# One-hot tables of a token router: five wide VectorE instructions per two chunks in place of twelve on GpSimd

## The chip, the cores and the metric

One core of a Trainium2 chip runs the whole program. Its engines each work through their own instruction queue in order and wait for each other by semaphores: TensorE (PE, and PEld for its weight loads), VectorE (DVE), ScalarE (ACT), GpSimd (POOL) and SyncE (SP, which here only starts DMAs). The metric is the device time of one execution in microseconds; the kernel before takes 539.12 us (median of three, 538.48 to 539.36).

## The reference

Three layers follow each other. The first is an mLSTM recurrence over 2 x 8 heads of 768 steps, the second a mixture of eight experts of which each token uses two, the third an MLP with a gated activation.

```python
for t in range(S):                       # B, H, S, D = 2, 8, 768, 40
    m_new = np.maximum(f_gate[:, :, t] + m, i_gate[:, :, t])
    f_stab, i_stab = np.exp(f_gate[:, :, t] + m - m_new), np.exp(i_gate[:, :, t] - m_new)
    C = f_stab * C + i_stab * outer(v_t, k_t);  n = f_stab * n + i_stab * k_t
    y[:, :, t] = sigmoid(o_t) * (C @ q_t) / np.maximum(np.abs(n @ q_t), 1.0)
x = y as 1536 tokens of 320
noisy = x @ w_gate + np.log1p(np.exp(x @ w_noise)) * noise
top2 = np.argpartition(-noisy, 2, axis=1)[:, :2]       # weights: softmax of the two
for e in range(8):                                     # F = 1024
    out[mask] += top2_w * (np.maximum(x[mask] @ w1[e], 0) @ w2[e])
h = out @ w_in;  result = (h * np.clip(h + 3, 0, 6) / 6) @ w_out      # 2048 wide
```

## The kernel before, in words

The 768 steps of both batches are cut into 12 chunks of 128 rows (64 steps of each batch). The loop from line 1077 walks over the chunks: it reads the state (`inter`), adds to it (`state`), makes scores two chunks ahead (`scores`), multiplies with the values (`values`, line 339), transposes the finished rows (`xpose`, line 412) and computes the router's logits (line 426). VectorE multiplies scores and decays into `P` (line 292), updates the state `Sb` (line 328), and finishes the chunk in `y`, `den`, `rd` and `x` (lines 358 to 384). GpSimd makes the decayed state `Sd` (line 301) and the gated output `od` (line 369).

For each pair of chunks a generator `route(m)`, m = 0 to 5, picks the two experts of each token and gives each token a place in its expert's list. It is cut by `yield` into small pieces; every call of `step()` in the main program runs each living generator up to its next yield, so the number of yields decides where its instructions stand in the engines' queues, between those of the main program. Some pieces wait until a counter `spot` has moved on.

A route counts tokens per expert by matmuls (lines 488 to 491), adds the base of each expert (`pe`, line 511), and turns the result into a slot number `sl`. The last part enters the tokens into a table of slots. The slot's low seven bits `lh[:, 0]` choose one of 128 rows, the others one of 32 columns. `LO` is the one-hot of the row (four choices of 128 each), `HV` the one-hot of the column times the token's number, in two parts (`pcol`, the row in the chunk, and `nval`, the chunk's first token). Four matmuls at line 562 multiply the two, and line 564 adds the result into `slot`. After m = 3 and after m = 5 the table is turned into indices `idx` (line 567), from which GpSimd gathers the tokens of the experts (`gather`, line 818).

Routes 0 to 4 make `LO` and `HV` on GpSimd, with twelve instructions whose comparands are per-partition scalars in `lf`, a float32 copy of `lh`. Route 5 makes them on VectorE with wide instructions that broadcast both operands. Routes 4 and 5 run beside the first expert unit, whose first layer is `L1` (line 891, evicted by ScalarE at 894 and VectorE at 897) and whose second is `L2` (lines 927 to 932). The weights come as float32 and are split in two parts, on ScalarE (line 641) and VectorE (line 642). From the first unit on TensorE goes through the experts and then the MLP.

Of the kernel before, what the change touches and what calls it, by code (L numbers as in the profile page):

```python
# [13 lines left out]
BF = mybir.dt.bfloat16  # L14
# [4 lines left out]
OP = mybir.AluOpType  # L19
# [3 lines left out]

B, H, S, D = 2, 8, 768, 40
NT = 12
DM = H * D
E = 8
# [39 lines left out]
def mlstm_moe_mlp(ctx, tc, qk, kv, on, gf, gf4, wg, nz, w1, w2, w_in, w_out, cf, cb, ci, out):  # L67
    nc = tc.nc
    V, A, G, T = nc.vector, nc.scalar, nc.gpsimd, nc.tensor
    const = ctx.enter_context(tc.tile_pool(name="const", bufs=1))  # L70
# [47 lines left out]
    def kv_part(n):  # L118
        kvt[n] = att.tile([128, H * (D + V1)], F32, name="kv", bufs=4)
        return kvt[n], kv[n]  # L120

    def load_qk(n, eng=nc.sync):
        for a in qk_parts(n):
            eng.dma_start(*a)

    def load_kv(n, eng=nc.sync):
        eng.dma_start(*kv_part(n))

    def load_on(n):
        nc.sync.dma_start(ont[:, n:n + 2], on[:, n:n + 2])  # L130
# [64 lines left out]
    def later_exponents():  # L195
        exponents(g64[:, 1], g64[:, 0], m64, 64, 1, R[:, 0], R[:, 1], R[:, 2])
        for sp in range(3):
            G.dma_start(RWG[sp * 32:sp * 32 + 16, 2:6].rearrange("p c x t -> p (c x t)"),
                        R[:, sp].rearrange("p c x t -> p (c x t)"))
        pre_cm.__exit__(None, None, None)  # L200
# [20 lines left out]
    iota128, pcol, nval = cft[:, 147:275], cft[:, 275:276], cft[:, 276:288]  # L221
# [21 lines left out]
    def step(k=1):  # L243
        for _ in range(k):
            for g_ in list(gens):
                if next(g_, "end") == "end":
                    gens.remove(g_)
# [6 lines left out]
    def scores(n, ps_=range(4)):  # L254
        q = QK[n % 4]
        if n not in s4t:
            s4t[n] = (itp if n == 1 else s4p)[:, :, 0:256].rearrange("p x (a t) -> p x a t", a=4)
        s4 = s4t[n]
        for p in ps_:
            for x in range(2):  # L260
                r = slice(64 * x, 64 * x + D)
                for b in range(B):
                    T.matmul(s4[rows[b], x, p, :], q[r, p, 1, rows[b]], q[r, p, 0, rows[b]], start=True, stop=True)
# [24 lines left out]
    def pmul(n):  # L288
        d = Pt[n][1]
        s4 = s4t.pop(n)  # L290
        P = att.tile([128, 8, 64], F32, name="P", bufs=3)
        V.tensor_tensor(P.rearrange("p (x a) t -> p x a t", x=2), s4, d.rearrange("p (x a) t -> p x a t", x=2), OP.mult)
        Pt[n] = P
# [10 lines left out]
    def inter(n, bp=5, two=itp):  # L304
        q = QK[n % 4]
        vv = kvt[n][:, DM:].rearrange("p (h d) -> p h d", h=8)
        pv = bank(bp)[:, 0:8 * V1].rearrange("p (h d) -> p h d", h=8)
        it = two[:, :, 0:4 * V1].rearrange("p x (a c) -> p x a c", a=4)
        for p in range(4 if n else 0):
            for x in range(2):  # L310
                r = slice(64 * x, 64 * x + D)
                for b in range(B):
                    T.matmul(it[rows[b], x, p, :], q[r, p, 0, rows[b]], Sb[r, b, p, :], start=True, stop=True)
        y_ps[n] = (pv, it, vv)

    def state(n):
        Sd = Sds.pop(n, None)
        vv = y_ps[n][2]
        for p in range(4):
            for b in range(B):  # L320
                for x in range(2):
                    h = 4 * x + p
                    T.matmul(stp[64 * x:64 * x + D, b, p, :], kt[n][rows[b], h, :],
                             vv[rows[b], h, :], start=True, stop=True)
        spot[0] += 2
        step(2)
        if n:
            V.tensor_tensor(Sb, Sd, stp, OP.add)
        else:
            V.tensor_copy(Sb, stp)  # L330
        step()
        if n + 2 < NT:
            decay(n + 1)

    def values(n, hs):
        pv, _, vv = y_ps[n]
        for h in hs:
            for b in range(B):
                T.matmul(pv[rows[b], h, :], Pt[n][rows[b], h, :], vv[rows[b], h, :], start=True, stop=True)
# [41 lines left out]
    def norm2(n):  # L381
        o, rd = yt[n]
        x = att2.tile([128, XW], F32, name="x", bufs=4)
        V.tensor_tensor(x[:, 0:DM].rearrange("p (a x d) -> p x a d", a=4, x=2), o.rearrange("p (x a) d -> p x a d", x=2),
                        rd.rearrange("p (x a) -> p x a", x=2)[:, :, :, None].to_broadcast([128, 2, 4, D]), OP.mult)
        A.copy(x[:, DM:XW], x[:, 256:DM])
        xt[n] = x
        nc.sync.dma_start(Xd[n * 128:(n + 1) * 128], x)
# [9 lines left out]
    SLE = const.tile([128, NT, 2], I32, name="SLE")  # L398
    SLY = const.tile([128, NT, 2], I32, name="SLY")
    WAB = const.tile([128, NT, 2], F32, name="WAB")  # L400
    run = const.tile([128, E], BF, name="run")
    V.memset(run, 0.0)
    adj = const.tile([128, E], F32, name="adj")
# [32 lines left out]
    def small(shape, name, dt=F32, bufs=2):  # L436
        return const.tile(shape, dt, name=name, bufs=bufs)

    def route(m):
# [41 lines left out]
        V.tensor_tensor(dl, mx[:, :, 1:2], mx[:, :, 0:1], OP.subtract)  # L481
        wab = WAB[:, 2 * m:2 * m + 2]
        e2 = small([128, 2, 1], "e2")
# [47 lines left out]
        lh = small([128, 2, 4], "lh", I32)  # L531
# [3 lines left out]
        V.scalar_tensor_tensor(lh[:, 1], sli, 7, h1, OP.bitwise_and, OP.bitwise_or)  # L535
        LO = small([128, 4, 128], "LO", BF, 1)
        HV = small([128, 4, 2, 32], "HV", BF, 1)
        if m < NT // 2 - 1:
            lf = small([128, 2, 4], "lf")
            V.tensor_copy(lf, lh)  # L540
            for j in range(4):
                G.tensor_scalar(LO[:, j], iota128, lf[:, 0, j:j + 1], None, OP.is_equal)
                for x, v in enumerate((pcol, nval[:, 2 * m + j // 2:2 * m + j // 2 + 1])):
                    G.tensor_scalar(HV[:, j, x], iota128[:, 0:32], lf[:, 1, j:j + 1], v, OP.is_equal, OP.mult)
        else:
            V.tensor_tensor(LO, iota128[:, None, :].to_broadcast([128, 4, 128]),
                            lh[:, 0, :, None].to_broadcast([128, 4, 128]), OP.is_equal)
            yield
            H = small([128, 4, 32], "H", BF, 1)
            V.tensor_tensor(H, iota128[:, None, 0:32].to_broadcast([128, 4, 32]),  # L550
                            lh[:, 1, :, None].to_broadcast([128, 4, 32]), OP.is_equal)
            yield
            V.tensor_scalar(HV[:, :, 0], H, pcol, None, OP.mult)
            V.tensor_tensor(HV[:, :, 1].rearrange("p (n k) c -> p n k c", n=2), H.rearrange("p (n k) c -> p n k c", n=2),
                            nval[:, 2 * m:2 * m + 2, None, None].to_broadcast([128, 2, 2, 32]), OP.mult)
        at = spot[0]
        yield
        while spot[0] < at + SPI and not now[0]:
# [208 lines left out]
    def w_lo(k=1):  # L767
        for _ in range(k):
            los.pop(0)()
# [33 lines left out]
    for i, u in enumerate(units):  # L803
        u.i = i
        u.g, u.xb = (i - M0) // 3, i % 2 if i < M0 else (i - M0) % 3
        n = len(u.tiles)
# [39 lines left out]
    def combine(u, i):  # L846
        n = 4 * (u.e - 8) + i
        t = ygt[n]
        x = late.tile([128, XW], F32, name="x2", bufs=2)
        A.mul(t[:, 0], t[:, 0], WAB[:, n, 0:1])  # L850
        V.scalar_tensor_tensor(x[:, 0:DM], t[:, 1], WAB[:, n, 1:2], t[:, 0], OP.mult, OP.add)  # L851
        V.scalar_tensor_tensor(x[:, DM:XW], t[:, 1, 256:DM], WAB[:, n, 1:2], t[:, 0, 256:DM], OP.mult, OP.add)
        x2t[n] = x
# [223 lines left out]
    for n in range(NT - 2):  # L1077
        pmul(n + 1)
        step(2)
        inter(n)  # L1080
        state(n)
        if n == 1:
            later_exponents()
            G.tensor_copy(adj, iota8)
        if n + 4 < NT:
            load_qk(n + 4)
        if 0 < n < NT - 3:
            load_kv(n + 3)
        if n % 2 == 0 and n + 2 < NT:
            load_on(n + 2)  # L1090
        if n >= 1:
            norm2(n - 1)
            step()
        w_lo(WL[n] if n < len(WL) else 0)
        scores(n + 2)
        values(n, range(8))
        if n >= 1:
            xpose(n - 1)
        expo(n + 2)
        for _ in range(WD[n] if n < len(WD) else 0):  # L1100
            w_load()
        w_hi(WH[n] if n < len(WH) else 0)
        if n == 1:
            decays(4, NT)
        if n + 3 >= NT:
            dummy(DUM[0], 4)
        if n >= 1:
            logits(n - 1)
        kscale(n + 2)
        if n == 0:  # L1110
            for i in range(3):
                gate(0, i)
        for i in ((0,), (1, 2))[n % 2]:
            gate(n // 2 * 2 + 2, i)
        norm_eg(n)
        step(2)
        norm_pv(n)
        if n >= 2 and n % 2 == 0:
            gens.append(route(n // 2 - 1))
    n = NT - 2  # L1120
# [152 lines left out]
    v, w = hbs  # L1273
# [75 lines left out]
```

## Time and profile before

| | |
|---|---|
| median of three runs | 539.12 us |
| profiled execution | 538.7 us |
| its span, from first to last instruction | 536.9 us |
| TensorE / VectorE / ScalarE / GpSimd busy | 494.1 / 341.1 / 231.7 / 129.2 us |
| mean granted TensorE clock | 0.892 |

Times within the trace are counted from the span's start. The profile's page gives shares over the whole span; the timeline gives the single instructions, with the idle time ahead of each in brackets and the instruction whose end ended it. A busy time of TensorE includes overlap, since its matmuls are pipelined. The granted clock is 1.00 at 2.4 GHz and 0.50 at 1.2 GHz. Line numbers are those of the kernel before, except in rows of the changed kernel, where a line behind the change stands one to three lines elsewhere.

### The profile page before, as it was taken

What the parts mean: (1) busy time and instruction counts of PE and PEld (TensorE: products, weight loads), DVE (VectorE), ACT (ScalarE), POOL (GpSimd) and SP (SyncE); (2) the same over time, 40 slices, a digit from 0 to 9 for tenths busy, and PEclk for the clock granted to TensorE, in tenths of its full rate; (3) what the DMA queues carried; (4) which work ended last, traced back from release to release, by engine and by line L of the source; (5) the groups of instructions that cost most, each with busy time, mean ns of one, the idle gap of its engine ahead of it and who ended that gap; (6) DMA issues with size and microseconds to landing.
All of it is one profiled execution on the core that took longest, in us unless ns stands there. A gap on an engine that the chain in (4) does not pass through costs nothing. (4 is left out here: it accounts for less than half of the span.)

```text
span 536.9 us, 11617 instructions
## 1 busy us (share of the span) xinstructions
PE 494.1 (92%) x4547; PEld 449.1 (84%) x4547; DVE 341.1 (64%) x874; ACT 231.7 (43%) x483; POOL 129.2 (24%) x178
## 2 busy tenths in 40 slices
PE   5799867868699999999999999989999999999996
PEld 2687656646699999999999999979989899899985
DVE  7547766727476587878787877468697434353433
ACT  2346547215254454545454553255564334333322
POOL 2434455263330420202111002377400100000000
PEclk9555555559699999999999999999999999999999
DMA  9858663233277479888988769697722600010011
GB/s 187 206 170 234 167 191 117 71 95 93 79 219 219 151 271 292 290 284 290 273 302 275 267 183 319 205 295 227 241 99 80 214 0 1 1 31 20 13 37 49
DMA packets 41531, 90.76 MB, mean 169 GB/s; under 512 B 5233, under 2 KB 23985, under 8 KB 41473
## 3 DMA queue, kind: packets, MB, share of 16 engines
q1 hardware_dynamic: 34960, 69.07, 41.1%
q0 software_dynamic: 5696, 19.67, 11.9%
q10 hardware_dynamic: 816, 1.25, 1.1%
q8 instruction: 36, 0.59, 0.5%
q14 instruction: 23, 0.18, 0.1%
HBM read 67.16 MB, written 22.68 MB: 167 GB/s over the span
## 5 line engine op out<-in xcount | busy, mean ns | idle before, releaser
L906 DVE SCALAR_TENSOR_TENSOR r<-r,bank 128x512 f32<-128x512 f32 (+1 forms) x56 | 34.2, 611 | 80.1 <-ACT r L905 79.6
L894 ACT ACTIVATE hb<-bank 128x416 fp32r<-128x416 f32 (+2 forms) x80 | 35.6, 446 | 95.9 <-PE bank L891 82.7
L905 ACT ACTIVATE r<-bank,cft 128x512 f32<-128x512 f32 (+1 forms) x56 | 35.0, 626 | 95.5 <-PE bank L891 92.3
L891 PE MATMUL bank<-XH,SB 128*128 128x416 f32 (+3 forms) x280 | 75.6, 340 | 0.3 <-PEq L991 0.3
L891 PE MATMUL bank<-XL,SB 128*128 128x416 f32 (+3 forms) x192 | 66.9, 349 | 0.0
L818 POOL DMA_INDIRECT XG<-Xd,idx x32 | 33.1, 1034 | 127.5 <-PE bank L828 116.7
L927 PE MATMUL bank<-SB,hb 128*128 128x320 f32 x192 | 61.9, 322 | 1.0 <-ACT hb L878 1.0
L927 PE MATMUL bank<-SA,hb 128*128 128x320 f32 x192 | 61.3, 319 | 0.0
L929 PE MATMUL bank<-SA,hb 128*128 128x320 f32 x192 | 59.7, 311 | 0.1
L928 PE MATMUL bank<-SA,hb 128*128 128x320 f32 x192 | 59.6, 310 | 0.0
L929 PE MATMUL bank<-SB,hb 128*128 128x320 f32 x192 | 59.3, 309 | 0.0
L928 PE MATMUL bank<-SB,hb 128*128 128x320 f32 x192 | 59.2, 308 | 0.0
L891 PEld LDWEIGHTS bank<-XH,SB 128*128 128x128 f32 x280 | 50.3, 189 | 4.6 <-issue 0.6
L891 PE MATMUL bank<-XH,SA 128*128 128x416 f32 (+2 forms) x200 | 51.2, 329 | 0.1
L891 PE MATMUL bank<-XL,SA 128*128 128x416 f32 (+2 forms) x120 | 39.3, 329 | 0.1
L891 PEld LDWEIGHTS bank<-XH,SA 128*128 128x128 f32 x200 | 36.5, 196 | 1.9 <-ACT XH L829 0.6
L927 PEld LDWEIGHTS bank<-SB,hb 128*128 128x128 f32 x192 | 36.2, 188 | 2.1 <-ACT hb L878 1.2
L891 PEld LDWEIGHTS bank<-XL,SB 128*128 128x128 f32 x192 | 36.2, 188 | 2.0
L927 PEld LDWEIGHTS bank<-SA,hb 128*128 128x128 f32 x192 | 36.4, 190 | 1.1
L928 PEld LDWEIGHTS bank<-SA,hb 128*128 128x128 f32 x192 | 36.4, 190 | 0.9
L928 PEld LDWEIGHTS bank<-SB,hb 128*128 128x128 f32 x192 | 36.2, 189 | 0.6
L929 PEld LDWEIGHTS bank<-SA,hb 128*128 128x128 f32 x192 | 36.3, 189 | 0.3 <-DVE hb L879 0.3
(225 smaller groups left out, 1113.8 us busy)
## 6 DMA issues: line engine op xcount, KB each, us to landing
raw<-in_w_dram SPq DMA_DIRECT2D x18, 640.0 KB, 4.8
raw<-in_w_dram SPq DMA_DIRECT2D x18, 512.0 KB, 5.6
craw<-in_w_in_dram SPq DMA_DIRECT2D x8, 640.0 KB, 6.4
craw<-in_w_out_dram SPq DMA_DIRECT2D x8, 640.0 KB, 6.4
raw<-in_w_dram SPq DMA_DIRECT2D x18, 256.0 KB, 4.3
qk<-in_qk_dram SPq DMA_DIRECT2D x22, 192.0 KB, 4.3
Yd<-yo SPq DMA_DIRECT2D x24, 160.0 KB, 4.6
kv<-in_kv_dram SPq DMA_DIRECT2D x11, 324.0 KB, 5.0
```

Source lines behind the costliest of these rows:

```text
L818: G.indirect_dma_start(out=XG[0:n, (u.xo + i) % 4, :], out_offset=None, in_=Xd[0:CUT[u.i] * 128] if early else Xd[:, :], in_offset=bass.In ...
L891: T.matmul(p, a, b, start=(i == 0), stop=(i == 7))
L894: A.activation(hb[:, 0:N], p, AF.Relu)
L905: A.activation(r, p, AF.Relu, bias=three)
L906: V.scalar_tensor_tensor(r, r, 6.0, p, OP.min, OP.mult)
L927: T.matmul(p, h, wh, start=s, stop=False)
L928: T.matmul(p, h, wl, start=False, stop=False)
L929: T.matmul(p, hb[:, lo:lo + n], wh, start=False, stop=t)
```

## The change

Routes 0 to 5 now all make the one-hots on VectorE. The ramp that they are compared with is copied once to bfloat16 (`iotab`, on GpSimd in the loop's second pass), `lf` becomes bfloat16, and each of the pieces has its own yield.

```diff
--- before.py
+++ after.py
@@ -398,6 +398,7 @@
     SLE = const.tile([128, NT, 2], I32, name="SLE")
     SLY = const.tile([128, NT, 2], I32, name="SLY")
     WAB = const.tile([128, NT, 2], F32, name="WAB")
+    iotab = const.tile([128, 128], BF, name="iotab")
     run = const.tile([128, E], BF, name="run")
     V.memset(run, 0.0)
     adj = const.tile([128, E], F32, name="adj")
@@ -535,24 +536,20 @@
         V.scalar_tensor_tensor(lh[:, 1], sli, 7, h1, OP.bitwise_and, OP.bitwise_or)
         LO = small([128, 4, 128], "LO", BF, 1)
         HV = small([128, 4, 2, 32], "HV", BF, 1)
-        if m < NT // 2 - 1:
-            lf = small([128, 2, 4], "lf")
-            V.tensor_copy(lf, lh)
-            for j in range(4):
-                G.tensor_scalar(LO[:, j], iota128, lf[:, 0, j:j + 1], None, OP.is_equal)
-                for x, v in enumerate((pcol, nval[:, 2 * m + j // 2:2 * m + j // 2 + 1])):
-                    G.tensor_scalar(HV[:, j, x], iota128[:, 0:32], lf[:, 1, j:j + 1], v, OP.is_equal, OP.mult)
-        else:
-            V.tensor_tensor(LO, iota128[:, None, :].to_broadcast([128, 4, 128]),
-                            lh[:, 0, :, None].to_broadcast([128, 4, 128]), OP.is_equal)
-            yield
-            H = small([128, 4, 32], "H", BF, 1)
-            V.tensor_tensor(H, iota128[:, None, 0:32].to_broadcast([128, 4, 32]),
-                            lh[:, 1, :, None].to_broadcast([128, 4, 32]), OP.is_equal)
-            yield
-            V.tensor_scalar(HV[:, :, 0], H, pcol, None, OP.mult)
-            V.tensor_tensor(HV[:, :, 1].rearrange("p (n k) c -> p n k c", n=2), H.rearrange("p (n k) c -> p n k c", n=2),
-                            nval[:, 2 * m:2 * m + 2, None, None].to_broadcast([128, 2, 2, 32]), OP.mult)
+        yield
+        lf = small([128, 2, 4], "lf", BF)
+        V.tensor_copy(lf, lh)
+        yield
+        V.tensor_tensor(LO, iotab[:, None, :].to_broadcast([128, 4, 128]),
+                        lf[:, 0, :, None].to_broadcast([128, 4, 128]), OP.is_equal)
+        yield
+        H = small([128, 4, 32], "H", BF, 1)
+        V.tensor_tensor(H, iotab[:, None, 0:32].to_broadcast([128, 4, 32]),
+                        lf[:, 1, :, None].to_broadcast([128, 4, 32]), OP.is_equal)
+        yield
+        V.tensor_scalar(HV[:, :, 0], H, pcol, None, OP.mult)
+        V.tensor_tensor(HV[:, :, 1].rearrange("p (n k) c -> p n k c", n=2), H.rearrange("p (n k) c -> p n k c", n=2),
+                        nval[:, 2 * m:2 * m + 2, None, None].to_broadcast([128, 2, 2, 32]), OP.mult)
         at = spot[0]
         yield
         while spot[0] < at + SPI and not now[0]:
@@ -1082,6 +1079,7 @@
         if n == 1:
             later_exponents()
             G.tensor_copy(adj, iota8)
+            G.tensor_copy(iotab, iota128)
         if n + 4 < NT:
             load_qk(n + 4)
         if 0 < n < NT - 3:
```

TensorE's queue, where route 0's slot matmuls (line 562, here the rows with LO) stood, before:

```order
L313 MATMUL itp<-Sb,qk_88 64x41 x16
L323 MATMUL itp<-kv,kt 40x41 x16
L562 LDWEIGHTS LO
L562 MATMUL bank_169<-HV,LO 128x64
L562 LDWEIGHTS LO
L562 MATMUL bank_169<-HV,LO 128x64
L562 LDWEIGHTS LO
L562 MATMUL bank_169<-HV,LO 128x64
L562 LDWEIGHTS LO
L562 MATMUL bank_169<-HV,LO 128x64
L263 MATMUL s4p<-qk_90 64x64 x16
L339 MATMUL bank_1013<-kv,P 64x41 x16
```

and in the changed kernel, at the same place:

```order
L427 MATMUL bank_170<-wgt,xT 32x16 x12
L313 MATMUL itp<-Sb,qk_88 64x41 x16
L323 MATMUL itp<-kv,kt 40x41 x16
L263 MATMUL s4p<-qk_90 64x64 x16
L339 MATMUL bank_1006<-kv,P 64x41 x16
L413 MATMUL bank_1089<-cft,x 128x128 x2
```

and one step later, where line 562 is 559 and line 488 is 489:

```order
L313 MATMUL itp<-Sb,qk_89 64x41 x16
L323 MATMUL itp<-kv,kt 40x41 x16
L559 LDWEIGHTS LO
L559 MATMUL bank_170<-HV,LO 128x64
L559 LDWEIGHTS LO
L559 MATMUL bank_170<-HV,LO 128x64
L559 LDWEIGHTS LO
L559 MATMUL bank_170<-HV,LO 128x64
L559 LDWEIGHTS LO
L559 MATMUL bank_170<-HV,LO 128x64
L489 LDWEIGHTS cbt
```

They moved from between the state matmuls (line 323) and the scores (line 263) of one step to behind the state matmuls of the next one; route 1 likewise. Those of routes 2, 4 and 5 keep their places.

VectorE's queue around the same place, before (line 451 is the route of the next pair, which waits for ScalarE's `u`; 564 the table):

```order
L535 SCALAR_TENSOR_TENSOR lh<-SL,h_978 128x4
L540 CAST lf<-lh 128x8
L377 RECIPROCAL rd<-den 128x8
L292 TENSOR_TENSOR P<-s4p,dd 128x512
L442 COPY zg<-bank_169 128x32
L451 TENSOR_SCALAR w<-u 128x16
L453 SCALAR_TENSOR_TENSOR w<-w,u 128x16
L564 TENSOR_TENSOR slot<-slot,bank_169 128x64
L455 SCALAR_TENSOR_TENSOR w<-zg,w 128x16
L328 TENSOR_TENSOR Sb<-Sd,itp 128x328
```

and in the changed kernel (lines 543 to 551 are the new instructions):

```order
L377 RECIPROCAL rd<-den 128x8
L541 CAST lf<-lh 128x8
L292 TENSOR_TENSOR P<-s4p,dd 128x512
L543 TENSOR_TENSOR LO<-iotab,lf 128x512
L443 COPY zg<-bank_170 128x32
L547 TENSOR_TENSOR H<-iotab,lf 128x128
L452 TENSOR_SCALAR w<-u 128x16
L550 TENSOR_SCALAR HV<-H,cft 128x4x32
L551 TENSOR_TENSOR HV<-H,cft 128x4x32
L454 SCALAR_TENSOR_TENSOR w<-w,u 128x16
L456 SCALAR_TENSOR_TENSOR w<-zg,w 128x16
L328 TENSOR_TENSOR Sb<-Sd,itp 128x328
```

The slot addition has left this stretch, and four wide instructions have come in, two ahead of `w` and two behind it; the addition now stands behind the `P` (line 292) of the next step.

TensorE's queue at the end of the recurrence, route 3, before:

```order
L339 MATMUL bank_1847<-kv,P 64x41 x16
L313 MATMUL s4p<-Sb,qk_90 64x41 x16
L562 LDWEIGHTS LO
L562 MATMUL bank_169<-HV,LO 128x64
L562 LDWEIGHTS LO
L562 MATMUL bank_169<-HV,LO 128x64
L562 LDWEIGHTS LO
L562 MATMUL bank_169<-HV,LO 128x64
L562 LDWEIGHTS LO
L562 MATMUL bank_169<-HV,LO 128x64
L339 MATMUL bank_1920<-kv,P 64x41 x16
L412 MATMUL bank_1989<-cft,x 128x128 x2
```

and in the changed kernel (lines 413 and 427 are lines 412 and 426 of before):

```order
L339 MATMUL bank_1828<-kv,P 64x41 x16
L313 MATMUL s4p<-Sb,qk_90 64x41 x16
L339 MATMUL bank_1901<-kv,P 64x41 x16
L413 MATMUL bank_1958<-cft,x 128x128 x2
L413 MATMUL bank_1958<-cft,x 64x128
L413 MATMUL bank_1977<-cft,x 128x128 x2
L413 MATMUL bank_1977<-cft,x 64x128
L427 MATMUL bank_170<-wgt,xT 32x16 x12
L559 LDWEIGHTS LO
L559 MATMUL bank_170<-HV,LO 128x64
L559 LDWEIGHTS LO
L559 MATMUL bank_170<-HV,LO 128x64
```

The values of the last chunk, two chunks' transposes and one chunk's logits now stand ahead of route 3's slot matmuls.

## Rows read from the trace of the kernel before

**Rows 1.** The page's slices of 13.4 us: granted TensorE clock in tenths.

```profile
PEclk9555555559699999999999999999999999999999
```

**Rows 2.** Two stretches: length, busy (instructions), clock, DMA, GB/s.

```profile
51.90:69.98 18.08, 14.65 (x350) 11.97 (x348) 12.84 (x51) 10.68 (x34) 8.80 (x15) 0.50 0.70 197
200.00:300.00 100.00, 100.00 (x623) 96.79 (x621) 81.67 (x166) 48.56 (x82) 14.69 (x15) 1.00 0.88 288
```

**Rows 3.** Waits, 40 to 160 us: who <- whom: us in total, times, longest.

```profile
PE bank L562 <- POOL HV L544: 24.8, 19, 2.7
...
DVE w L451 <- ACT u L446: 12.1, 5, 2.9
DVE slot L564 <- PE bank L562: 12.1, 4, 5.6
...
DVE pe L511 <- PE bank L491: 3.5, 3, 2.1
...
DVE t L499 <- PE bank L495: 0.7, 1, 0.7
```

**Rows 4.** Groups by form, 40 to 150 us: busy, mean ns, idle.

```profile
L544 POOL TENSOR_SCALAR HV<-cft,lf 128x32 bf16<-128x32 f32 x40 | 18.4, 469 | 0.0
...
L542 POOL TENSOR_SCALAR LO<-cft,lf 128x128 bf16<-128x128 f32 x20 | 12.8, 640 | 8.9 <-DVE lf L540 7.3 <-DVE rd L377 1.1 <-DVE den L374 0.4
```

**Rows 5.** Timeline, 44 to 62 us, TensorE: start, us, instruction [idle].

```profile
51.95 0.77 PE L323 MATMUL itp<-kv,kt 64*40 64x41 f32 x32
...
56.87 1.13 PE L263 MATMUL s4p<-qk 40*64 40x64 f32 x32
```

**Rows 6.** The same timeline, VectorE.

```profile
54.95 0.17 DVE L451 TENSOR_SCALAR w<-u 128x16 f32<-128x16 f32 x1 [2.88 <-ACT u L446]
...
56.98 0.22 DVE L564 TENSOR_TENSOR slot<-slot,bank 128x64 f32<-128x64 f32 x1 [1.61 <-PE bank L562]
```

**Rows 7.** Timeline, 96 to 150 us, TensorE.

```profile
105.28 1.14 PE L313 MATMUL s4p<-Sb,qk 40*64 40x41 f32 x30
...
113.36 1.93 PE L339 MATMUL bank<-kv,P 64*64 64x41 f32 x32
...
123.44 0.38 PE L891 MATMUL bank<-XH,SA 128*128 128x256 f32 x1
...
131.70 0.31 PE L929 MATMUL bank<-SA,hb 128*128 128x320 f32 x1
...
139.33 0.56 PE L891 MATMUL bank<-XH,SA 128*128 128x256 f32 x1
...
141.68 0.61 PE L927 MATMUL bank<-SA,hb 128*128 128x320 f32 x1
...
143.43 0.41 PE L891 MATMUL bank<-XH,SA 128*128 128x256 f32 x1
...
145.40 0.39 PE L927 MATMUL bank<-SA,hb 128*128 128x320 f32 x1
...
146.37 0.29 PE L562 MATMUL bank<-HV,LO 128*128 128x64 bf16 x4
```

**Rows 8.** Timeline, 96 to 150 us, VectorE.

```profile
132.04 1.23 DVE L642 TENSOR_TENSOR SB<-raw,SB 128x1024 fp32r<-128x1024 f32 x1
...
139.51 0.22 DVE L564 TENSOR_TENSOR slot<-slot,bank 128x64 f32<-128x64 f32 x1 [5.91 <-PE bank L491]
...
141.94 0.69 DVE L546 TENSOR_TENSOR LO<-cft,lh 128x512 bf16<-128x512 f32 x1
...
142.87 0.29 DVE L550 TENSOR_TENSOR H<-cft,lh 128x128 bf16<-128x128 f32 x1
...
143.76 0.28 DVE L554 TENSOR_TENSOR HV<-H,cft 128x128 bf16<-128x128 bf16 x1
```

**Rows 9.** Timeline, 96 to 150 us, GpSimd.

```profile
132.31 1.44 POOL L542 TENSOR_SCALAR LO<-cft,lf 128x128 bf16<-128x128 f32 x1 [7.33 <-DVE lf L540]
...
138.21 0.91 POOL L544 TENSOR_SCALAR HV<-cft,lf 128x32 bf16<-128x32 f32 x2
```

## Prediction

> **What bounds the kernel now.** I read four views in this order. First the page's clock by slices [rows 1] and the busy times of two stretches [rows 2]: from 200 to 300 us TensorE is busy for 100.00 of 100.00 us, so the expert stage is bound by TensorE itself, and a microsecond won before it should reach the end of the program. In the recurrence before it nothing is full: in the 18.08 us of one pair of steps TensorE is busy for 14.65 and VectorE for 12.84, at a granted clock of 0.50. Second, the waits between 40 and 160 us [rows 3]: the longest of all is TensorE at line 562 (the four matmuls that add two chunks to the slot table), which waits for GpSimd's HV, 24.8 us in 19 waits. Third, the costs of the two groups it waits for [rows 4]: 40 HV at 469 ns and 20 LO at 640 ns, together 31.2 us for five routes, 6.2 us a route, serial on GpSimd and released by the last one. Fourth, the timelines. TensorE takes its instructions in order: after the state matmuls at 51.95 it could start the scores of a later chunk, and starts them at 56.87 [rows 5], because the slot matmuls stand between. VectorE's slot addition, and behind it the state update Sb, wait as well: 1.61 us here [rows 6], 12.1 us over four routes [rows 3]. Call the routes m = 0 to 5: m = 0 to 2 run inside the recurrence, m = 3 at its end, m = 4 and 5 beside the first expert unit; m = 5 had its one-hots on VectorE already.
>
> **The change, part by part.** It takes 60 instructions off GpSimd and puts four wide ones on VectorE for each of five routes (the fifth, the cast lf, was there). Route m = 5 shows three of the four forms: LO 0.69, H 0.29, the second HV 0.28 us [rows 8]; I count the first HV like the second, so 1.54 us a route. These sources are float32 and int32 and the new ones bfloat16, which no row shows. As bounds I take twice these durations from above, and from below 0.28 for LO as well, since no row of a wide instruction here is shorter; I keep 1.54, the nearest row.
>
> The Trainium skill (VectorE: DVE Perf Modes, What auto-detection actually checks) lets a two-source instruction take its double rate only where every tensor is 16-bit with a step of one. The lf operand here is broadcast with step 0 along the row, so by that rule the bfloat16 copy of the ramp wins nothing and LO stays near the 0.69 of the row; no run here shows it yet.
>
> The cast iotab on GpSimd, once, stands before the routes and has the size of one LO, 0.64 us [rows 4] (bounds 0 and that): GpSimd waits for its inputs there, cost 0.
>
> **Routes 0 to 2.** On TensorE the slot matmuls of m = 0 and 1 now stand one step later, behind the next state matmuls, those of m = 2 where they were. So TensorE's wait goes, but VectorE is next. It has two things to do in a step that TensorE waits for (Sb for the state, P for the values), and it gets its own wait back, not TensorE's. What it gets back: the slot waits, 12.1 less the 5.6 of m = 3 = 6.5 us; and what it waits for TensorE at the counts (pe 3.5 in three, t 0.7 in one [rows 3]), less the first of these before any one-hot, some 0.7: 3.5 us. What it pays: in m = 0 and 1 LO and H stand ahead of the instruction w, which waits 2.88 us for ScalarE anyway [rows 6], so they are hidden; if that wait were shorter than 0.98 they would count. The two HV stand behind w and count, 0.56 each time. In m = 2 LO stands ahead of P and counts, 0.69, and I add 0.56 for what follows. Together 6.5 + 3.5 - 0.56 - 0.56 - 1.25 = 7.6 us.
>
> **Route 3.** TensorE stands from 106.4 (the end of the row at 105.28, 1.14 long) to 113.36, 6.9 us [rows 7], less four slot matmuls of some 0.1 each: 6.5 at most. Now values, two transposes and logits stand ahead of the slot matmuls, and one transpose needs x of chunk 10, which VectorE makes behind LO, H and both HV. VectorE's own wait for slot is the 5.6 [rows 3]; less 1.54 it is 4.1 at least. Behind it come the table idx and the first gather. I take 5.0, between the two and nearer the lower, since the chain to the gather runs through VectorE.
>
> **Route 4.** TensorE ends at 132.0, and the last HV of GpSimd at 139.1 [rows 7, 9]. On VectorE the four stand where the weight split L642 began, 132.04 [rows 8]; they end near 133.6, and the slot matmuls run 5.5 us earlier. There is a second gain. While TensorE stood, its granted clock fell: the six matmuls from 141.68 to 143.43 took 1.75 us, the same six from 145.40 to 146.37 took 0.97 [rows 7]. With a gap of 1.6 us in place of 7 I expect the full clock to last, so that the 7.0 us from 139.33 to 146.37 hold some 4.4 us of work: 2.6 gained. Against it, VectorE now stands 1.54 further back with L642 (1.23) and an eviction, and route 5 follows at once. From the slot addition to the end of route 5's HV it took 4.5 us (139.5 to 144.0); with L642 ahead it takes 5.8, so route 5's matmuls come near 133.6 + 0.5 + 5.8 = 139.9 and not at 138.2, 1.7 us given back. 5.5 + 2.6 - 1.7 = 6.4.
>
> **Sum.** 7.6 + 5.0 + 6.4 = 19.0 us. The profiled execution took 538.7 us (span 536.9 and 1.8 around it), 0.4 below the median of the three; so 538.7 - 19.0 = 519.7 us. ScalarE's and SyncE's orders are unchanged; weight loads are released by the splits and move with them.
>
> **The rivals.** (a) All of TensorE's wait goes: 24.8 + 2.6 = 27.4, 511.3 us. For it speaks that VectorE is idle for 5 of 18 us. Against it, that this idle time lies in waits for ScalarE (12.1 at w) and that VectorE's busy 12.84 + 1.54 already comes near TensorE's 14.65 for the pair. 0.13.
>
> (b) VectorE takes the recurrence over: the wide instructions cost twice the rows (3.1 us a route) or meet GpSimd's own od and Sd, and routes 0 to 2 give nothing: 5.0 + 6.4 = 11.4, 527.3 us. For it, row 132.31: a GpSimd LO took 1.44 us beside VectorE's L642 at 132.04, where its group's mean is 0.64 [rows 4, 8, 9]. Against it, that od and Sd wait for VectorE's results and run where VectorE is past the one-hots. 0.14.
>
> The Trainium skill (SBUF — State Buffer, Who interferes with whom) says that a VectorE instruction with two SBUF inputs and a GpSimd instruction that reads SBUF block each other, the first to start holding the port to its end; the row at 132.31 agrees. LO, H and one HV have two inputs, 1.26 us a route: if each held GpSimd on the path in five routes it would take back 6.3 us.
>
> (c) Slower: TensorE's clock. It was granted 0.50 all through the recurrence and full only just before the first expert matmul at 123.44 [rows 1, 7]. If the dense stretch that raised it is broken now by the wait for the gather, the first units run at 1.2 GHz, where work takes 1.75 us in place of 0.97. Each us of work at the full clock then costs 0.8 more; from some 24 us of such work on (19.0 / 0.8) all is lost, and 30 us would give 538.7 - 19.0 + 24 = 543.7 us. Against it: the instructions that stood before the rise stand there still, and TensorE has less idle time ahead of them. 0.03.
>
> (d) It does not do what it says: TensorE waits as long, now for HV on VectorE behind w. The moved slot matmuls speak against it. 538.7 us, 0.02.
>
> **How the numbers follow.** Forecast 0.68, (a) 0.13, (b) 0.14, (c) 0.03, (d) 0.02. The forecast's own range is the sum of its ends: routes 0 to 2 from 5 to 9, route 3 from 4.1 to 6.5, route 4 from 4 to 8: 13 to 23.5, 515 to 526. The range of 8 in 10 reaches a little towards (a) and (b): 512.5 to 527. This kernel's measurement can tell some 0.2%, 1.1 us, from no change. Faster by more than that are the forecast, (a) and (b), 0.95; within it (d), 0.02; slower (c), 0.03.
>
> **What would show it.** In the changed profile: line 562's matmuls no longer wait for GpSimd, and their waits sum to under 5 us; VectorE has no wait for the slot matmuls of routes 0 to 2; the first expert matmul starts near 111, not 123.4; the clock does not fall between it and route 5's matmuls; route 5's wait of 1 to 2 us is new; LO is near 0.69 us. The prediction is wrong if the step of the recurrence does not shorten where the slot matmuls stood, or if VectorE's P or Sb comes as late as before.

## The result, and the profile after

The changed kernel took 519.44 us (median of 4 runs, 519.02 to 519.72) beside 539.19 us (538.48 to 539.36) for the kernel before: 0.9635 of it, with a 95% interval of 0.9619 to 0.9652. The forecast was 519.7. A second set gave 518.95 beside 539.08, 0.9616 (0.9601 to 0.9631). The profiled execution took 519.53 us, its span is 517.7 us.

The page's clock by slices answers to [rows 1]: the recurrence is still granted about half of the clock, and from the tenth slice of 12.9 us on it stays at nine tenths or more; before, the eleventh fell back to 0.6.

```profile
PEclk9555555579999999999999999999999999999999
```

Two stretches, in the columns of [rows 2] (length, then busy time of TensorE, its loads, VectorE, ScalarE and GpSimd, the clock, DMA):

```profile
50.00:68.00 18.00, 16.43 (x358) 13.06 (x356) 14.71 (x59) 11.15 (x35) 3.85 (x5) 0.50 0.80 220
200.00:300.00 100.00, 99.70 (x619) 95.96 (x618) 80.29 (x160) 51.35 (x85) 12.64 (x12) 1.00 0.83 277
```

In 18 us of the recurrence TensorE is now busy for 16.43 (before 14.65) and GpSimd for 3.85 (before 8.80). The expert stage is as it was: TensorE is full, so what is won ahead of it stays won.

The waits from 38 to 135 us, to be read beside [rows 3]:

```profile
DVE w L452 <- ACT u L447: 8.8, 5, 2.1
...
PE bank L559 <- DVE HV L551: 3.7, 3, 1.4
...
PE bank L825 <- DMA XG<-Xd,idx: 1.8, 2, 1.5
...
DVE slot L561 <- PE bank L559: 0.3, 1, 0.3
```

TensorE's 24.8 us for GpSimd's HV are 3.7 us for VectorE's. VectorE's 12.1 us at the slot addition are 0.3, and they stand at route 3; routes 0 to 2 have none.

The four new groups on VectorE, by form (busy, mean ns):

```profile
L543 DVE TENSOR_TENSOR LO<-iotab,lf 128x512 bf16<-128x512 bf16 x6 | 4.1, 683 | 0.0
L551 DVE TENSOR_TENSOR HV<-H,cft 128x128 bf16<-128x128 bf16 x6 | 1.7, 284 | 0.0
L547 DVE TENSOR_TENSOR H<-iotab,lf 128x128 bf16<-128x128 bf16 x6 | 1.6, 273 | 0.0
L550 DVE TENSOR_SCALAR HV<-H,cft 128x128 bf16<-128x128 bf16 x6 | 1.5, 250 | 0.1
```

TensorE's timeline after, at the places of [rows 5 and 7] (start, us, instruction, idle time and what ended it):

```profile
53.70 0.74 PE L323 MATMUL itp<-kv,kt 64*40 64x41 f32 x27
...
62.64 0.40 PE L559 MATMUL bank<-HV,LO 128*128 128x64 bf16 x4
...
79.40 1.13 PE L263 MATMUL s4p<-qk 40*64 40x64 f32 x32 [0.41 <-DVE P L292]
...
87.27 0.37 PE L559 MATMUL bank<-HV,LO 128*128 128x64 bf16 x4 [0.97 <-DVE HV L551]
...
96.09 0.20 PE L489 MATMUL bank<-mk,cbt 128*128 128x16 bf16 x1
...
110.80 0.58 PE L888 MATMUL bank<-XH,SA 128*128 128x256 f32 x1
...
121.03 0.28 PE L559 MATMUL bank<-HV,LO 128*128 128x64 bf16 x4 [1.45 <-DVE HV L551]
...
127.13 0.28 PE L559 MATMUL bank<-HV,LO 128*128 128x64 bf16 x4 [1.32 <-DVE HV L551]
```

These starts, and the same ones of the other kernels, cut the program into stages that can be compared. The marks are: the state matmul beside which route 0 stood before (51.95 before, 53.70 after); the scores behind route 1; the count matmul of route 3; the first expert matmul; the last slot matmul of route 4; that of route 5; the end of the span. Each column is the time from the mark before it, in us, in the profiled execution.

| kernel | routes 0, 1 | route 2 | route 3 | route 4 | route 5 | to the end |
|---|---|---|---|---|---|---|
| before | 30.85 | 20.63 | 20.01 | 15.73 | 7.20 | 390.5 |
| after | 25.70 | 16.69 | 14.71 | 10.23 | 6.10 | 390.6 |
| after, again | 25.71 | 16.69 | 15.28 | 10.18 | 6.10 | 391.5 |
| e1 place only | 25.60 | 20.65 | 17.09 | 15.74 | 6.47 | 391.6 |
| e2 engine only | 25.52 | 16.80 | 15.41 | 10.18 | 5.51 | 394.6 |
| e3 route 4 on GpSimd | 25.70 | 16.68 | 15.28 | 15.76 | 7.26 | 391.5 |
| e5 HV ahead of w | 25.23 | 16.80 | 15.33 | 10.17 | 6.10 | 390.4 |
| e6 LO twice | 25.70 | 17.41 | 17.34 | 11.15 | 6.83 | 393.7 |
| e8 as e3, filled | 25.70 | 16.68 | 14.41 | 15.75 | 5.16 | 392.4 |
| e9 later split | 25.69 | 16.69 | 15.18 | 12.26 | 6.16 | 389.9 |

From before to after the columns give 5.15 + 3.94 + 5.30 + 5.50 + 1.10 = 21.0 us. The first mark itself comes 1.75 later, so 19.2 arrive at the end. 0.5 to 0.6 of the 1.75 lie ahead of 46 us; the rest stands around the first row here, a stall of TensorE for nothing that the profile shows ("issue" in the idle column). The second row, of the same kind, lies behind the mark:

```profile
48.45 1.93 PE L339 MATMUL bank<-kv,P 64*64 64x41 f32 x31 [0.86 <-issue]
...
54.83 0.37 PE L323 MATMUL itp<-kv,kt 64*40 64x41 f32 x5 [0.38 <-issue]
```

The second profile of the same kernel has no such stall (its first mark is at 52.71), so not every execution has it. Five of the twelve profiles of the changed kernel and its variants show it, and the one profile of the kernel before does not; whether the change has a part in it stays open.

### The profile page after: what moved, and what is told of

Its sections match the earlier page's. It is cut to its first block, busy times and chain, and to the rows that moved or that the text cites. A ratio compares the mean times of both kernels' runs of the same rounds, so it can differ in the third digit from the quotient of the medians.

```text
span 517.7 us, 11574 instructions
## 1 busy us (share of the span) xinstructions
PE 490.1 (95%) x4544; PEld 446.7 (86%) x4547; DVE 345.8 (67%) x895; ACT 232.0 (45%) x483; POOL 99.6 (19%) x119
## 3 DMA queue, kind: packets, MB, share of 16 engines
q10 hardware_dynamic: 816, 1.25, 1.1%
## 5 line engine op out<-in xcount | busy, mean ns | idle before, releaser
L924 PEld LDWEIGHTS bank<-SA,hb 128*128 128x128 f32 x192 | 36.1, 188 | 1.1
L925 PEld LDWEIGHTS bank<-SA,hb 128*128 128x128 f32 x192 | 36.1, 188 | 0.9
L897 DVE SCALAR_TENSOR_TENSOR hb<-bank,hb 128x32 fp32r<-128x32 f32 x64 | 12.0, 188 | 36.6 <-ACT hb L891 36.5
```

The costliest lines, as they stand in the source:

```text
L897: V.scalar_tensor_tensor(hb[:, N:N + u.tail], p[:, o:N], 0.0, hb[:, o:N], OP.max, OP.subtract)
L924: T.matmul(p, h, wh, start=s, stop=False)
L925: T.matmul(p, h, wl, start=False, stop=False)
```

## The experiments

Chips differ by up to 0.5% (the kernel before took 538.3, 541.2 and 539.1 us beside three sets), so totals are given as ratios to the kernel before on the same chip, and as the difference of the medians there. The changed kernel is 19.75 and 20.13 us below it in its two sets. The ratio and the difference of the medians can part by about 1 us; where that matters, both are given. Lines in the rows are those of each run's own kernel: the slot matmuls are line 571 in e1 and e3, 573 in e8, 555 in e2, and 559 in e9.

**The place alone** (e1). TensorE's order is that of the changed kernel; the one-hots of routes 0 to 4 are made on GpSimd as before (shortened; the four yields of the change stay in).

```
+ if m < NT // 2 - 1:
+     lf = small([128, 2, 4], "lf")            # float32
+     for j in range(4):
+         G.tensor_scalar(LO[:, j], iota128, lf[:, 0, j:j + 1], ...)
+         for x, v in enumerate((pcol, nval...)):
+             G.tensor_scalar(HV[:, j, x], iota128[:, 0:32], lf[:, 1, j:j + 1], v, ...)
```

> The place alone: routes 0 to 4 make their one-hots on GpSimd with the twelve small instructions of the kernel before, while the code's steps, and with them TensorE's order, are those of the changed kernel (route 5 stays on VectorE). Theory 1: what counts is where the slot matmuls stand in TensorE's order and how long after the slots they get their HV. Then routes 0 and 1, whose matmuls stand one step later, keep their gain, also without the HV cost on VectorE, some 6.2 us; route 2 (matmuls in their old place, GpSimd as late as before) gives about 0; route 3 gives 2 to 3; route 4 gives 0, because GpSimd ends as late as before and the clock falls in the gap: 538.7 - 8.7 = 530, 528 to 533. Theory 2: only the engine counts, GpSimd's one-hots being late for any place: about 538.5.

Measured: 531.5 us (530.66 to 532.55), 6.8 below the kernel before, 0.9865 (0.983 to 0.9899). Theory 2 is out. Its timeline on TensorE:

```profile
60.56 0.40 PE L571 MATMUL bank<-HV,LO 128*128 128x64 bf16 x4
...
89.38 0.21 PE L571 MATMUL bank<-HV,LO 128*128 128x64 bf16 x1 [1.27 <-POOL HV L547]
```

The four slot matmuls of route 0 run without a wait although GpSimd made the one-hots: one step later they are simply there. The table has routes 0 and 1 at 25.60, as in the changed kernel; route 2, which did not move, at 20.65, as before; route 3 won 2.9 and route 4 nothing, as expected. The expected sum of 8.7 is met by 8.9 up to route 5's matmuls; 6.8 of it is there in the total.

**The engine alone** (e2). The four added steps of the code are taken out, so that the slot matmuls of routes 0 to 4 stand in their old places, with the one-hots on VectorE.

```
-        yield
         lf = small([128, 2, 4], "lf", BF)
         V.tensor_copy(lf, lh)
-        yield
...
-        yield
...
-        yield
```

> The engine alone: the one-hots on VectorE as in the changed kernel, but LO, H and both HV in one piece and without the four new steps of the code, so that the slot matmuls of routes 0 to 4 stand where they stood in TensorE's order before. Theory 1 (the place counts in routes 0 and 1): the slot matmuls of routes 0 and 1 still stand ahead of the scores and TensorE waits for VectorE there, for the whole piece; routes 0 and 1 lose most of their gain of some 5.5 us, the rest stays: 523 to 527. Theory 2 (the engine counts): four VectorE instructions take 1.54 us a route where GpSimd took 6.2, so even in the old place the wait is short, and the time is that of the changed kernel, 518 to 522.

Measured: 521.61 us (520.65 to 522.15), 16.7 below, 0.9673 (0.9639 to 0.9706): within the range of theory 2, some 2 to 3 us short of the changed kernel. But not for the reason of theory 1: routes 0 and 1 take 25.52, no more than in the changed kernel. Either part of the change gives the whole gain of these two routes; only route 2 and behind need the engine. What is missing lies behind route 5. There TensorE's last four slot matmuls stand earlier in its order, and it waits longer for VectorE:

```profile
125.08 0.37 PE L555 MATMUL bank<-HV,LO 128*128 128x64 bf16 x4 [2.88 <-DVE HV L547]
```

The stretches around it (the clock is the third figure from the end) show the clock falling in that gap, for some 6 us of work that at the full clock takes about half:

```profile
122.00:124.00 2.00, 0.20 (x2) 0.00 (x0) 1.93 (x6) 0.98 (x1) 0.00 (x0) 1.00 0.66 242
124.00:126.00 2.00, 0.92 (x7) 1.03 (x8) 1.96 (x8) 0.00 (x0) 0.00 (x0) 0.53 0.65 190
...
128.00:130.00 2.00, 2.00 (x10) 2.00 (x10) 0.81 (x3) 0.47 (x1) 1.58 (x2) 0.50 0.40 123
```

**Route 4 alone back on GpSimd** (e3). The edit of e1 under `if m == 4`.

> The changed kernel with route 4 alone back on GpSimd (twelve small instructions). Theory 1: route 4 is worth 5.5 us of time gained by its earlier one-hots and 2.6 of clock, less 1.7 of new waits: TensorE stands some 7 us ahead of route 4's slot matmuls again, its granted clock falls in that stretch, and the time is 519.5 + 6.4 = 526, 524.5 to 528. Theory 2: what route 4 gains is given back at route 5 or hidden by the first expert unit: 519.5 to 521, and the granted clock stays full.

Measured: 524.53 us (523.37 to 525.96), 13.8 below, 0.9722 (0.9687 to 0.9757). That is 6.0 us less gained than by the changed kernel if the medians are taken, and 4.7 by the ratios, whose interval here is 3.8 us wide; 6.4 was expected. The table has it in routes 4 and 5: 15.76 + 7.26 against 10.18 + 6.10.

**The same with the gap filled** (e8). 28 filler matmuls stand ahead of route 4's slot matmuls, where TensorE waits for GpSimd.

```
         pi = pz[:, 128:192]
+        if m == 4:
+            dummy(28, 4)
```

> The kernel of e3 (route 4 on GpSimd), with 28 filler matmuls (128x128 by 128x512, bfloat16, constants, some 6 us at the full clock) ahead of route 4's slot matmuls, in the 7.3 us in which TensorE waits for GpSimd there. It tells the clock from the wait. Theory 1: the clock falls because TensorE stands; with the fillers it stays at 1.00, the work behind takes its time at the full clock, and then route 5 is set by VectorE, 6.1 us behind route 4 as in the changed kernel and not 7.3: 1.2 less than e3, 523.3, 522.5 to 524. Theory 2: the clock's whole 2.6 us come back: 521.9. Theory 3: the fillers win nothing, because the work behind waits for VectorE anyway: 524.5 or a little more.

Measured: 525.69 us (524.22 to 527.05) on the slowest of the chips, 15.5 below, 0.9721 (0.9693 to 0.975). In the total it can't be told from e3: the ratios are equal, and the 1.7 us between the differences lie inside the intervals. The trace tells it up to route 5. First e3, then e8, from 124 to 128 us:

```profile
124.00:126.00 2.00, 0.73 (x8) 0.68 (x8) 0.24 (x3) 0.00 (x0) 1.37 (x3) 0.50 0.00 0
126.00:128.00 2.00, 2.00 (x12) 2.00 (x11) 2.00 (x12) 0.33 (x1) 0.00 (x0) 0.50 0.03 8
```

```profile
124.00:126.00 2.00, 1.01 (x12) 1.11 (x13) 0.70 (x7) 0.00 (x0) 0.94 (x3) 1.00 0.00 0
126.00:128.00 2.00, 2.00 (x18) 2.00 (x17) 2.00 (x9) 1.65 (x3) 0.00 (x0) 1.00 0.00 0
```

With TensorE kept busy the clock stays at 1.00 behind the same wait, and route 5 follows after 5.16 us instead of 7.26. So 2.1 us of the 7.26 were the clock's, and TensorE's work there is 2.6 us shorter, since in e8 it waits 0.46 for VectorE's HV at route 5 and in e3 not at all. What of it reaches the end this pair does not settle.

**Both HV ahead of w** (e5). LO, H and HV in one piece, two steps moved behind it.

```
-        yield
         H = small([128, 4, 32], "H", BF, 1)
...
-        yield
         V.tensor_scalar(HV[:, :, 0], H, pcol, None, OP.mult)
...
+        yield
+        yield
```

> The changed kernel with LO, H and both HV in one piece (two code steps moved behind it), so that in routes 0 and 1 both HV stand ahead of the instruction w on VectorE, which waits for ScalarE there, and not behind it. Theory 1 (in the recurrence the cost is what VectorE does behind w): 0.56 us less in each of two routes, 518.4, 517.8 to 519. Theory 2 (VectorE has slack behind w and the step is set by ScalarE and TensorE): no change, 519.4. Theory 3 (the piece delays w, because ScalarE's wait leaves less room than the 1.54): some 0.5 slower, 520.

Measured: 518.7 us (517.27 to 519.09), 19.6 below, 0.9612 (0.9578 to 0.9646): as a total not to be told from the changed kernel. The table has 25.23 for routes 0 and 1 against 25.71, 0.48 for two routes where theory 1 had 1.12. VectorE's instructions show why, first in the changed kernel, then in e5:

```profile
53.65 0.68 DVE L543 TENSOR_TENSOR LO<-iotab,lf 128x512 bf16<-128x512 bf16 x1
...
56.71 0.17 DVE L452 TENSOR_SCALAR w<-u 128x16 f32<-128x16 f32 x1 [2.08 <-ACT u L447]
56.80 0.25 DVE L550 TENSOR_SCALAR HV<-H,cft 128x128 bf16<-128x128 bf16 x1
56.96 0.29 DVE L551 TENSOR_TENSOR HV<-H,cft 128x128 bf16<-128x128 bf16 x1
...
57.46 0.49 DVE L328 TENSOR_TENSOR Sb<-Sd,itp 128x328 f32<-128x328 f32 x1
```

```profile
56.29 0.17 DVE L452 TENSOR_SCALAR w<-u 128x16 f32<-128x16 f32 x1 [1.59 <-ACT u L447]
...
56.80 0.49 DVE L328 TENSOR_TENSOR Sb<-Sd,itp 128x328 f32<-128x328 f32 x1
```

From the start of w to that of the state update Sb it is 0.75 us in the changed kernel and 0.51 in e5, so a pair of HV behind w costs 0.24. The second HV starts 0.16 behind the first, which is shown as 0.25 long: the durations of neighbours overlap, and their sum is not their cost.

**LO twice** (e6).

```
+        V.tensor_tensor(LO, iotab..., lf..., OP.is_equal)      # once more
```

> The changed kernel with LO computed twice in each of the six routes, one more VectorE instruction of 0.6 to 0.69 us a route. Theory 1 (what VectorE does ahead of w is hidden in routes 0 and 1, where w waits 2.1 us for ScalarE; in routes 2, 4 and 5 TensorE waits for HV and pays; route 3 pays half): 3.5 times 0.6 = 2.1 slower than the changed kernel, 521.5, 520.7 to 522.3. Theory 2 (VectorE is the bound in every route): six times 0.62 = 3.7, 523.1. Theory 3 (VectorE's work is hidden everywhere): 519.4.

Measured: 524.58 us (521.93 to 526.92), 16.6 below, 0.9677 (0.9645 to 0.9708), 3.2 to 3.5 us less gained than by the changed kernel by the medians, 2.3 by the ratios (0.9677 against 0.9635). The table shows where a microsecond of VectorE counts: nothing in routes 0 and 1 (25.70), 0.7 in route 2, 1.0 and 0.7 in routes 4 and 5. Route 3 is 2.1 longer, and of that 1.3 is a longer wait for the gather's data (2.14 us in place of 0.81), which differs from execution to execution too. Theory 1 has the places right, but route 3 pays some 0.8 beside the gather and not half of 0.6; its sum of 2.1 lies inside the interval of the total. The profiled execution was the slowest of the four (526.92). In the waits, what is hidden comes out of VectorE's own wait for ScalarE, 5.8 where the changed kernel has 8.8:

```profile
DVE w L452 <- ACT u L447: 5.8, 5, 1.5
```

**A float32 ramp** (e4). LO and H from iota128 and a float32 lf, without the cast iotab.

```
-        lf = small([128, 2, 4], "lf", BF)
+        lf = small([128, 2, 4], "lf")
-        ... iotab[:, None, :] ...  iotab[:, None, 0:32]
+        ... iota128[:, None, :] ...  iota128[:, None, 0:32]
```

> The changed kernel with float32 sources: LO and H are compared against the float32 ramp iota128 and a float32 lf, and the cast iotab is gone. Theory 1: the price of LO does not hang on the bfloat16 copy of the ramp, since the lf operand is broadcast along the row; LO stays 0.67 to 0.69 us as route 5 showed in the kernel before, and the time stays 519.4, 518.8 to 520. Theory 2: the bfloat16 sources make LO and H cheaper than float32 ones, so that this one is slower by 0.2 to 0.4 us in each route that is not hidden: 520.5 to 521.

Measured: 521.24 us (520.6 to 521.6), 19.9 below, 0.9627 (0.9608 to 0.9647): the same as the changed kernel, and so is LO:

```profile
L543 DVE TENSOR_TENSOR LO<-cft,lf 128x512 bf16<-128x512 f32 x6 | 4.1, 682 | 0.0
```

**A weight split on GpSimd** (e7, e9, e10). VSPLIT names the pieces of a weight that GpSimd splits in VectorE's place.

```
-VSPLIT = {}
+VSPLIT = {1: "GVVV"}      # e7, on e5;  {1: "VGVV"} in e9 (on the changed kernel) and e10 (on e5)
```

> The order of e5 (both HV ahead of w), and the one weight split that stands behind route 4's one-hots (1.22 us on VectorE, the low halves of the second expert's first piece) is made by GpSimd, which is idle for 16.5 us there. Theory 1: from the first expert unit to route 5 VectorE is the bound (busy 1.8 to 2.0 of every 2 us from 112 to 128), so 1.22 us off it bring route 5 and the end forward by 0.8 to 1.2: 517.6, 517 to 518.3. Theory 2: another chain sets route 5 (ScalarE's activations or TensorE): 518.7 as with e5. Theory 3: a split on GpSimd holds up VectorE's instructions with two inputs while it runs (over 2 us by the mean of its 128x320 subtractions, 0.83): slower than e5, 519.5 to 521.

e7 did not do what its expectation says. The piece that it moved stands at 111 us, not behind route 4's one-hots. 523.06 us (519.91 to 523.64), 18.1 below, 0.9651 (0.9623 to 0.9679). Its profiled execution is late ahead of that split already (a wait of 2.47 us for the gather), so it decides nothing. e9 and e10 move the right piece, beside the changed kernel itself:

> The changed kernel itself once more, as the level for the two kernels beside it on the same chip, and to see whether TensorE's stall ahead of the first route (1.2 us, in no wait that the profile shows) belongs to it: 0.9635 of the kernel before, 0.962 to 0.965.

> The changed kernel, with the weight split that stands right behind route 4's one-hots on VectorE (1.22 us at 120.89) made by GpSimd; e7 had moved the split ahead of it, at 111, where VectorE still has idle time. Theory 1: from 118 to 128 VectorE is never idle and sets route 5, so all behind the split comes 1.1 us earlier: 1.1 us less than the changed kernel beside it. Theory 2: the split on GpSimd (2.39 us in e7) runs beside route 4's LO, H and HV, and holds up VectorE's instructions with two inputs: no gain or up to 1 us slower. Theory 3: ScalarE or TensorE sets route 5: the same time.

> The order of e5 (both HV ahead of w) and the split of e9 on GpSimd, the version that the experiments point to. Theory 1: the two gains add, 0.5 of e5 and 1.1 of e9: 1.6 us less than the changed kernel beside it. Theory 2: neither is to be told from the changed kernel: within 0.6 us of it.

Measured on one chip: the changed kernel 518.95 (0.9616, 0.9601 to 0.9631), e9 521.21 (519.74 to 523.31; 0.9677, 0.9653 to 0.9701), e10 519.89 (518.55 to 520.53; 0.9632, 0.9617 to 0.9648). Nothing is gained, as theory 2 of e9 says, but what is held up is not a one-hot instruction with two inputs (LO takes 0.69 us in e9 too). GpSimd, then VectorE, then TensorE in e9:

```profile
117.17 2.37 POOL L639 TENSOR_TENSOR SB<-raw,SB 128x1024 fp32r<-128x1024 f32 x1 [6.25 <-issue]
```

```profile
117.30 2.26 DVE L528 CAST SL<-sl 128x4 int32<-128x4 f32 x1
```

```profile
121.91 0.28 PE L559 MATMUL bank<-HV,LO 128*128 128x64 bf16 x4 [3.68 <-DVE HV L551]
```

The same cast in the changed kernel beside it:

```profile
118.06 0.17 DVE L528 CAST SL<-sl 128x4 int32<-128x4 f32 x1
```

GpSimd stands idle for 6.25 us for nothing that the profile shows and then starts the split, in the middle of VectorE's chain to route 4's one-hots and not behind them. A cast of four numbers a row, elsewhere 0.17 us long, then lasts to GpSimd's end. TensorE waits 3.68 us in place of 1.60, and its clock falls (0.50 from 124 to 126 us, where the changed kernel has 1.00). The Trainium skill (SBUF — State Buffer, Who interferes with whom) says that a VectorE cast can, in a two-port mode, contend with GpSimd for a shared pair of ports, and that the one to issue first has the pair for its whole instruction while the other is blocked. These two rows agree: the split ends at 119.54 us, the cast at 119.56.

By the medians e9 is 2.3 us slower than the changed kernel, where theory 2 had up to 1. But its runs reach from 519.74 to 523.31, and the profiled one, among the lowest, spans 518.0 us against 518.2: the 2.1 us lost in route 4 come back behind route 5 (389.9 against 391.5 in the table). What makes the other runs longer no trace shows.

e10 is 0.9 us above the changed kernel by the medians, with intervals that overlap: nothing won. Its trace has the same cast at 2.26 us, and TensorE waits 3.57 us at route 4. No kernel here is measurably faster than the changed one.

## Why the prediction was right

**What was to be seen is there.** The slot matmuls' waits sum to 3.7 us (forecast under 5), none for GpSimd; VectorE has no slot wait in routes 0 to 2; the first expert matmul starts at 110.80 (near 111); LO is 0.683 (near 0.69); route 5 waits 1.32 (1 to 2); and the clock, full from 112.7 us on, holds through both gaps:

```profile
120.00:122.00 2.00, 0.97 (x14) 1.07 (x15) 1.97 (x5) 0.20 (x1) 0.00 (x0) 1.00 0.00 0
...
126.00:128.00 2.00, 0.87 (x10) 0.96 (x11) 1.96 (x8) 0.00 (x0) 0.00 (x0) 1.00 0.64 242
```

**Routes 0 to 2: forecast 7.6, measured 9.1** (5.15 + 3.94). The mechanism holds: TensorE's wait goes, and VectorE with ScalarE sets the step. What was mis-sized is the price of VectorE's work. The stretch from the first mark to the count of route 3, before and after (VectorE's busy time is the third of the busy times):

```profile
51.95:103.43 51.48, 38.76 (x889) 30.83 (x885) 33.38 (x130) 27.65 (x86) 25.50 (x44) 0.50 0.51 146
```

```profile
53.70:96.09 42.39, 36.92 (x890) 30.34 (x885) 36.08 (x142) 27.77 (x86) 8.90 (x10) 0.50 0.58 171
```

VectorE's idle time falls from 18.1 to 6.3 us, by 11.8: 6.5 at the slot additions, as forecast; 2.7 at the counts, where 3.5 was forecast (the last one still waits 0.8); 2.6 at w, where 0.98 twice was to be hidden. Its busy time rises by 2.7, where the forecast's prices make 4.3 (1.54 twice and 1.25): 11.8 less 2.7 is 9.1. Of the 1.6 us between 4.3 and 2.7, e5 finds 0.6 in the HV pairs of routes 0 and 1, 0.24 each in place of 0.56; the rest is not put down to single instructions. LO is hidden in routes 0 and 1 and counts in route 2, as the prediction had it; e6 shows both. The argument also leaned on the moved matmuls more than it had to: e1 and e2 show that the move alone or the engine alone gives all of routes 0 and 1.

**Route 3: forecast 5.0, measured 5.3** (4.7 in the second profile). This stage holds a gather whose landing differs by a microsecond or so between executions, so the agreement is no finer than that.

**Route 4, and 5 behind it: forecast 6.4, measured 6.6.** The 5.5 for the earlier one-hots is 5.50 in the table. The rest was 2.6 of clock less 1.7 of new waits, 0.9 net, and is 1.10. From the last slot matmul of route 4 to route 5's TensorE took 7.20 us before, without a wait; after, it takes 6.10, of which 1.32 are the wait for VectorE's HV (row 127.13), so the work itself took 4.8. The clock gave 2.4 and the new wait cost 1.3: both terms were too large, by 0.2 and 0.4, and the errors partly cancel. e8 has the same work at the full clock in 4.7 (5.16 less a wait of 0.46). e3 agrees in the total, 4.7 to 6.0 us less gained.

**The sum.** 21.0 us measured in the stages against 19.0, less a later start of 1.75 and 0.1 behind route 5: 19.2 arrive. In the second profile the stages give 20.5, the start costs 0.8 and the stretch behind route 5 is 1.0 longer: 18.7 arrive. So the closeness to 519.7 is in part luck: the stages gave 1.5 to 2.0 us more than the forecast, and about as much was lost outside them, in each execution at another place.

**The rivals.** (a), that all of TensorE's wait goes, is out: new waits of 3.7 us and VectorE's work in routes 2, 4 and 5 stand in its place. (b), that VectorE takes over or is shut out by GpSimd: not for the one-hots, where LO takes 0.67 to 0.69 us in all six routes. But the two engines do meet. Beside GpSimd's od a small VectorE instruction that takes 0.17 us at 98.91 takes 0.81 in the changed kernel; in the stretch above its five have a mean of 551 ns before and after, so the change neither brought this nor took it away. e9 shows such a meeting on the path. GpSimd and VectorE in the changed kernel:

```profile
61.50 0.83 POOL L369 TENSOR_TENSOR od<-ont,y 128x320 f32<-128x320 f32 x1 [2.46 <-DVE ix L470]
```

```profile
61.56 0.81 DVE L372 TENSOR_SCALAR den<-y 128x8 f32<-128x8 f32 x1
```

Rival (c), the clock: the dense stretch ahead of the first expert matmul was broken by the wait for the gather (1.5 us), and the first few expert matmuls did run at the half clock (0.58 at 110.80, against 0.38 in [rows 7]), but the full clock was back by 112.7. e2 had it full there and was no faster in that stage (10.18 us in the table), at whose end TensorE waits 1.61 us for VectorE's HV. (d) is out. The changed kernel's clock at the first expert matmuls:

```profile
110.00:112.00 2.00, 2.00 (x8) 1.18 (x6) 0.87 (x3) 1.44 (x2) 1.70 (x2) 0.50 0.23 51
```

The rule on 16-bit operands that the prediction cites from the Trainium skill (VectorE: DVE Perf Modes, What auto-detection actually checks) agrees with the rows: e4 has LO at 682 ns from float32 and the changed kernel 683 from bfloat16.

## What to carry to other kernels

Where an engine that runs its instructions in order waits for a helper, ask both how late the helper is and how early the waiting instruction stands; here, in routes 0 and 1, either answer alone removed the wait, and the later place cost nothing. Price a run of small VectorE instructions by the starts of what stands before and behind it, not by the sum of their durations, and ask for each whether it stands ahead of a wait that hides it. Idle time on GpSimd is not free to use: work moved there starts at another time than on the engine it left, and here it held up the chain that it was meant to relieve.

## What the runs showed of the hardware

Beside a GpSimd subtraction of 2.37 us a VectorE cast took 2.26 us in place of 0.17 (e9, e10), and beside one of 0.83 us a small VectorE instruction took 0.81 in place of 0.17. In the expert stage TensorE's granted clock stayed at 1.00 through waits of 1.3 to 1.6 us (the changed kernel, e2), and fell to 0.50 behind waits of 2.2 (e6), 2.9 (e2) and 3.7 us (e9) and in the gap of e3, four waits of together 6.5 us; in e8, 28 filler matmuls in that gap kept it at 1.00. Ahead of that stage it rose to 1.00 (106 to 108 us in the changed kernel), and behind a wait of 1.5 us for the gather it fell again, to 0.50 from 110 to 112 us; in e8, where that wait was 1.1 us, it stayed at 1.00.
